# Moving two choosing matmuls of a sigmoid attention and mixture-of-depths kernel: the first sequence's to an earlier gap, the seventh's behind two products

## The chip, the cores and the metric

The kernel runs on one core of a Trainium2 chip. Its time is the device time of that core in microseconds. Three runs of the kernel before gave 466.89, 468.31 and 469.23 us; the median is 468.31 us. All arithmetic is in 32-bit floats.

The engines are named as in the profile: PE is TensorE (matmuls; PEld are its weight loads), DVE is VectorE, ACT is ScalarE, POOL is GpSimd, SP is SyncE, which only issues transfers. Each engine works through its own list of instructions in the order in which the program emits them, and waits where an operand or a buffer isn't ready.

## The reference

There are B=8 sequences of S=448 tokens, with 12 heads of 64. Attention with a sigmoid instead of a softmax gives x, one row of D=768 numbers for each token. Then a gate scores each token, the 128 tokens of each sequence with the highest scores go through a two-layer network, and the others are passed on as they are.

```python
scores = scale * np.matmul(q, k.transpose(0, 1, 3, 2)) - np.log(S)
attn = 1.0 / (1.0 + np.exp(-scores))
x = np.matmul(attn, v)            # then (B,H,S,D) -> (B, S, H*D)
...
scores = np.einsum('bsd,d->bs', x, w_gate)
out = x.copy()
for b in range(B):
    top_idx = np.argpartition(-scores[b], capacity)[:capacity]   # capacity 128
    xe = x[b, top_idx]
    h = np.maximum(xe @ w1, 0.0)  # w1: 768 x 1024
    ye = h @ w2                   # w2: 1024 x 768
    g = 1.0 / (1.0 + np.exp(-scores[b, top_idx]))
    out[b, top_idx] = x[b, top_idx] + g[:, None] * ye
```

## The kernel before

**Attention.** Four heads make a group, three groups a sequence, two groups a step: 12 steps `s`, so that sequence b ends in step (3b+2)//2. A step has seven units `n`. `unit(s, n)` (L287) computes a piece of the scores with 32 matmuls into two of PE's accumulation banks, and ACT takes them through the sigmoid. `values(s, n)` (L327) multiplies with v, in four parts: the first in unit 6 of the step itself, the others in the gaps after units 0, 1 and 2 of the next step. Its results stand in two banks `o0` and `o1`; after the last part `take` (L360) has DVE transpose them into `x_b`, four transposes for a step. In steps 1 to 3 unit 4 uses `o0` and `o1` for its scores too, between two steps' outputs. There are two further banks `psc`, which units use otherwise.

**Choosing the tokens.** `gate_part` (L370) multiplies x by the gate's weights and sums, four DVE operations for a group. When a sequence's three groups are done, `gate(b)` (L389) adds them up and POOL writes the 448 scores to memory (`scores`); `spread(b)` (L411) has POOL read them back to every partition (`rep`). `ranking(b)` (L667) compares every score with all others on DVE, ten operations in all, and `place` builds the matrix `hot` from the ranks. `choose(b)` (L438), the *choosing matmuls*, multiplies `hot` with the tokens' numbers and scores: four matmuls, eight PE instructions, into one bank. `fetch(b)` (L447) has DVE take the numbers (`idx`) and the scores (`got`) from that bank, and POOL gathers the chosen rows from `out` with an indirect transfer. The rows of the sequence were written to `out` before that by four stores on SP (`store`, L379), which `routed` (L649) places; those of sequence 0 are emitted at (2, 4), (2, 5.5), (2, 6) and (3, 0), step and unit.

**The network.** `turn_rows` (L468) turns the gathered rows round on PE. The two layers are computed for pairs of sequences in seven products each instead of eight (Strassen's scheme): `first` (L509) has 12 matmuls for a product, 24 PE instructions, and its sums (L532 and others) are DVE's.

**Order.** Nothing is planned by a scheduler: `stream` (L762) emits every instruction, so each engine's order is the program's. `gap(s, n)` (L684) holds what follows unit n: parts of `values`, then the network's work from the table `WORK`, then what `put` has left in `late`, then in gap 3 the second group's gate products and `gate`. For sequence 0 the scores are spread at (2, 4), the ranking is at (3, 1), and choice and fetch at (3, 5); for sequence 1 `gate` is in gap (3, 3), the spread at (3, 4) and the ranking at (4, 1), ahead of step 3's transposes in gap (4, 2). After unit 5 of steps 1 to 3 `keep_busy` (L319) has PE do some matmuls whose result nobody uses, into the bank that `open_outs` takes for the step's outputs.

**Banks.** `banks("o")` (L76) gives `o0` and `o1` in turn, `banks("any")` a `psc` bank and an `o` bank in turn, so that among four allocations each bank comes once. An allocation waits until the bank's last reader is done.

**The tail.** `rest` (L711) follows the last step. It emits the last parts of `values` with their transposes, the choice and fetch for sequence 6, products 6 and 7 of the third pair, the last group's gate products, `gate(7)`, the spread, the sums of products 6 and 7, then products 4, 5 and 3, second-layer products, `ranking(7)`, and so on to the end.

Of the kernel before, what the change touches and what calls it, by code (L numbers as in the profile page):

```python
# [17 lines left out]
def kernel(  # L18
# [22 lines left out]
    NG = H // 4  # L41
    NQ = B * NG
    NS = NQ // 2
# [32 lines left out]
    def banks(which):  # L76
        if which == "any":
            turns[1] ^= 1
            which = "psc" if turns[1] else "o"
        if which == "psc":  # L80
            return ps_sc.tile([P, 2, 512], F32, name="psc")
        if which == "o":
            turns[0] ^= 1
            which = turns[0]
        return ps_o[which].tile([P, 2, 512], F32, name=f"o{which}")
# [107 lines left out]
    def attn_tile(pr, slot):  # L193
        return attnp.tile([P, 2, S], F32, name=f"attn{pr}_{slot}")

    def lend(m, key, slot):


        halves = []
        for pr in range(2):  # L200
            if slot == "raw":
                t = raw.tile([P, TB * Dh], F32, name=f"raw_{'kq'[pr]}")[:, :QW // 2]
            elif slot == "turned":
                t = head.tile([P, 2, TB, TT], F32, name=f"{'kq'[pr]}T")
                t = t.rearrange("p e r t -> p (e r t)")[:, :QW // 2]
            else:
                t = attn_tile(pr, slot).rearrange("p a s -> p (a s)")[:, :QW // 2]
            nc.sync.dma_start(out=t, in_=sums[m, key][:, pr * QW // 2:(pr + 1) * QW // 2])
            halves.append(t)
        lent[m, key] = halves  # L210
# [104 lines left out]
    def open_outs(s):  # L315
        if s not in outs:
            outs[s] = [banks(0), banks(1)]

    def keep_busy(s):  # L319


        open_outs(s)
        for _ in range(3 if s == 3 else 4):
            nc.tensor.matmul(outs[s][0][:, 0, :HP * TT], iden,  # L324
                             wg_b.rearrange("p h t -> p (h t)"), start=True, stop=True)

# [43 lines left out]
    def gate_part(i):  # L370
        b, g = divmod(i, NG)
        for hp in range(2 * g, 2 * g + 2):
            tmp = moe.tile([P, TB, TT], F32, name="scr")
            nc.vector.tensor_tensor(  # L374
                out=tmp, in0=x_tiles[b][:, :, hp, :],
                in1=wg_b[:, hp:hp + 1, :].to_broadcast([P, TB, TT]), op=ALU.mult)
            nc.vector.tensor_reduce(out=gate_parts[b][:, :, hp], in_=tmp, axis=AX.X, op=ALU.add)  # L377

    def store(b, parts=range(4)):  # L379

        view = out[b].rearrange("(t r) (h a d) -> a t r h d", r=TB, a=4, d=TT)
        for a in parts:
            nc.sync.dma_start(out=view[a], in_=x_tiles[b][a * TT:(a + 1) * TT])

    def rows_to(b):

        return out[:b + 1].rearrange("b s d -> (b s) d")
# [50 lines left out]
    def choose(b, ps=None):  # L438

        if ps is None:  # L440
            ps = banks("o")[:, 0]
        for c in range(NC):
            nc.tensor.matmul(ps[:CAP, :2], st[b]["hot"][:, c, :CAP], who[b % 2][:, c, :],  # L443
                             start=(c == 0), stop=(c == NC - 1))
        return b, ps

    def fetch(b, ps):  # L447
        n = CAP
        idx = moe.tile([P, 1], I32, name="idx", bufs=5)
        nc.vector.tensor_scalar(out=idx[:n], in0=ps[:n, 0:1], scalar1=float(b * S),  # L450
                                scalar2=None, op0=ALU.add)
        got = moe.tile([P, 1], F32, name="got", bufs=4)
        nc.vector.tensor_copy(got[:n], ps[:n, 1:2])
        if b == B - 1:
            xe = attn_tile(0, f"u{NU - 1}").rearrange("p a s -> p (a s)")[:, :D]
        else:
            xe = moe.tile([P, D], F32, name="xe", bufs=3)
        nc.gpsimd.indirect_dma_start(
            out=xe[:n], out_offset=None, in_=rows_to(b),
            in_offset=bass.IndirectOffsetOnAxis(ap=idx[:n, 0:1], axis=0))  # L460
        st[b].update(idx=idx, xe=xe, picked=got)
# [3 lines left out]
    def bank(where):  # L465
        return banks(where)[:, 0]
# [163 lines left out]
    def begin(item, where="o"):  # L630

        m, p, key = item
        return (first if m == 1 else second)(p, key, where)

    def finish(item, args):
        (first_sums if item[0] == 1 else second_sums)(*args)

    def do(item, where="o"):
        if item[0] == "t":
            turn_rows(item[1], where)  # L640
        else:
            finish(item, begin(item, where))
# [3 lines left out]
    def put(s, n, fn, *args):  # L646
        late.setdefault((s, n), []).append((fn, args))

    def routed(b):  # L649

        s = (NG * b + NG - 1) // 2 + 1
        if s == NS:
            return
        put(s, 4, spread, b)
        if b < 2:

            parts = ((4, 0), (4, 1.5), (4, 3), (4, 4)) if b else (
                (2, 4), (2, 5.5), (2, 6), (3, 0))
            for a, at in enumerate(parts):
                put(*at, store, b, (a,))  # L660
        else:
            put(s, 4, store, b)
        put(s + 1, 1, ranking, b)
        if s + 1 < NS:
            put(s + 1, NU - 2, lambda b: fetch(*choose(b)), b)

    def ranking(b):  # L667
# [4 lines left out]
    def gates(i):  # L672
        gate_part(i)
        b, g = divmod(i, NG)
        if g == NG - 1:
            st[b] = {}
            waiting.append(b)

    def turned_next(s):

        m, x = WORK.get((s, 3), ((None, 0),))[0][:2]
        return m == "t" and x % 2 == 1

    def gap(s, n):  # L684
        if n < 3 and s > 0:
            values(s - 1, n + 1)
            if n == 2:
                turns[0] = 1
                for i, (m, key) in enumerate(LENT.get(s, ())):
                    lend(m, key, f"d{(s + 1) % 2}{i}")  # L690
                if not turned_next(s):
                    gates(2 * s - 2)
        for item in WORK.get((s, n), ()):
            do(item)
        if n == 3 and turned_next(s):
            gates(2 * s - 2)
        if n == 4 and turned_next(s):
            gate(waiting.pop())
            gates(2 * s - 1)
        if n == NU - 1 and s < NS:  # L700
            values(s, 0)
        for fn, args in late.pop((s, n), ()):
            fn(*args)
        if n == 3 and s > 0 and not turned_next(s):
            if waiting:
                gate(waiting.pop())
            gates(2 * s - 1)
            if waiting:
                gate(waiting.pop())

    def rest():  # L711


        for n in range(3):
            gap(NS, n)
        p, b = NP - 2, B - 1
        fetch(*choose(b - 1))
        for key, slot in (((2, 6), "d10"), ((2, 7), "d11")):
            lend(*key, slot)
        work = [(item, begin(item, "any")) for item in ((1, p, 6), (1, p, 7))]  # L720
        gates(2 * NS - 1)

        store(b, (0, 1))
        gate(waiting.pop())
        spread(b, nc.sync)
        store(b, (2, 3))
        for item, args in work:
            finish(item, args)
        for key in (4, 5):
            do((1, p, key), "any")  # L730
        first_sums(*begin((1, p, 3), "any"), sums_too=(5, 6))
        work = {key: begin((2, p, key), "any") for key in (2, 1, 4)}
        ranking(b)
        tile5 = banks("any")
        work[5] = second(p, 5, ps=tile5[:, 0])
        chosen = choose(b, tile5[:, 1])
        second_sums(*work[2])
        hidden_sum(p, 7)
        work[6] = begin((2, p, 6), "any")
        fetch(*chosen)  # L740
        second_sums(*work[1])
        hidden_sum(p, 3)
        work[7] = begin((2, p, 7), "any")
        for key in (4, 5, 6, 7):
            second_sums(*work[key])
        do(("t", b - 1), "any")
        do((2, p, 3), "any")
        p += 1
        for item in ((1, p, 1), ("t", b), (1, p, 2)):
            do(item, "any")  # L750
        work = [((1, p, key), begin((1, p, key), "any")) for key in (3, 6, 7)]
        for item, args in work[1:]:
            finish(item, args)
        first_sums(*work[0][1], sums_too=())
        for key in (4, 5):
            do((1, p, key), "any")
        for m in (5, 6, 7, 3):
            hidden_sum(p, m)
        for key in (1, 2, 6, 5, 3, 7, 4):
            do((2, p, key), "any")  # L760
# [76 lines left out]
```

## Time and profile before

One execution under the profiler spans 467.6 us.

| Engine | busy us | share of the span |
|---|---|---|
| PE, matmuls | 451.3 | 97% |
| PE, weight loads | 281.9 | 60% |
| DVE | 293.3 | 63% |
| ACT | 181.8 | 39% |
| POOL | 32.7 | 7% |

The transfers: 63.28 MB are read and 20.46 MB written, 179 GB/s over the span. On the chain of work that ended last PE has 85%, DVE 8% and transfers 3%.

How to read it: a row of the groups or the timeline gives the line of the kernel, the engine, the operation and the tiles as out<-in, then how often (x) and how long. "Idle before <-" says how long the engine had stood still and whose event ended that. Busy shares are means over stages of different kinds; what a change in one stage is worth is read from that stage. The windows view gives for a stretch of time the busy microseconds of each engine with the number of instructions, then the clock that was granted to PE (1.00 is full speed), the share of the transfer engines, and GB/s. Times in a view count from the start of the span.

### The profile page before, as it was taken

To read this page: it belongs to the slowest core of one execution; us is meant where nothing else is said; L and a number is where in the kernel's file an instruction comes from. 1 tells how busy PE (TensorE), PEld (TensorE's weight loads), DVE (VectorE), ACT (ScalarE), POOL (GpSimd) and SP (SyncE) were. 2 spreads that over 40 slices of the span, in tenths; PEclk is the share of its full clock that TensorE was granted. 3 is DMA by queue.
4 is the path that set the end of the run, shared out by engine and by line. 5 is a ranking of instruction groups with operands and counts; after the bars stand their busy time and mean duration, and the time that the engine had idled before them with its cause. 6 is when DMAs were issued, how large, how long until landed. Compare 5 with 4: busy or idle time off the path is not lost.

```text
span 467.6 us, 14444 instructions
## 1 busy us (share of the span) xinstructions
PE 451.3 (97%) x6412; PEld 281.9 (60%) x6412; DVE 293.3 (63%) x631; ACT 181.8 (39%) x237; POOL 32.7 (7%) x54
## 2 busy tenths in 40 slices
PE   8999999979999999999999999999999998999994
PEld 3464745434576755576456764676465738869952
DVE  4308769985642895984643795894742858685372
ACT  3846464624545345324445435324255520102000
POOL 6000000010000000010010000010010001001001
PEclk9999999979999999999999999999999998999998
DMA  8897997989753995994764973993823999611001
GB/s 269 220 313 185 342 347 149 264 197 302 165 193 116 207 192 185 204 215 153 173 227 148 153 202 118 228 213 132 220 102 98 222 181 328 106 34 69 2 0 67
DMA packets 128334, 84.67 MB, mean 181 GB/s; under 512 B 97600, under 2 KB 112064, under 8 KB 128272
## 3 DMA queue, kind: packets, MB, share of 16 engines
q1 hardware_dynamic: 126288, 75.84, 62.2%
q0 software_dynamic: 1984, 7.91, 5.7%
q8 instruction: 50, 0.82, 0.8%
q14 instruction: 12, 0.10, 0.1%
HBM read 63.28 MB, written 20.46 MB: 179 GB/s over the span
## 4 chain that ended last, share of the span: by engine, by line
PE 85%; DVE 8%; DMA 3%; issue 1%; ACT 1%; POOLq 0%; DVEq 0%; ACTq 0%
PE o L351 26%; PE psc L303 23%; PE o L519 13%; PE o L584 11%; PE psc L519 4%; PE psc L584 3%; DVE x_b L366 2%; PE o L303 2%; DMA scores<-total 1%; DVE gate_p L377 1%; DVE scr L374 1%; PE o L775 1%; PE o L443 1%; DMA rep<-scores 1%; PE o L324 1%
## 5 line engine op out<-in xcount | busy, mean ns | idle before, releaser
L303 PE MATMUL psc<-qT,kT 32*64 32x448 f32 x2496 | 155.1, 546 | 0.9 <-ACT attn_u L311 0.9
L311 ACT ACTIVATE attn_u<-psc,bias_s 128x896 f32<-128x896 f32 x86 | 81.9, 1004 | 94.6 <-PE psc L303 94.5
L351 PE MATMUL o<-attn_u,raw_v 32*64 32x448 f32 x960 | 107.8, 536 | 0.8 <-ACT o L354 0.8
L351 PE MATMUL o<-attn_d,raw_v 32*64 32x448 f32 x960 | 106.8, 536 | 0.4 <-ACT o L354 0.4
L303 PEld LDWEIGHTS psc<-qT,kT 32*64 32x64 f32 x2496 | 65.2, 133 | 56.4 <-issue 36.0
L311 ACT ACTIVATE attn_d<-psc,bias_s 128x896 f32<-128x896 f32 x70 | 66.7, 1003 | 47.9 <-PE psc L303 47.9
L366 DVE STREAM_TRANSPOSE x_b<-o 128x448 f32<-128x448 f32 x48 | 26.9, 618 | 81.5 <-PE o L351 77.3
L351 PEld LDWEIGHTS o<-attn_u,raw_v 32*64 32x64 f32 x960 | 45.6, 132 | 20.4 <-issue 12.5
L351 PEld LDWEIGHTS o<-attn_d,raw_v 32*64 32x64 f32 x960 | 43.9, 132 | 18.8 <-issue 14.8
L519 PEld LDWEIGHTS o<-rows_t,w_sb 128*128 128x128 f32 x264 | 30.4, 192 | 4.5 <-issue 1.4
L519 PEld LDWEIGHTS o<-rows_t,attn_d 128*128 128x128 f32 x264 | 30.3, 192 | 3.9 <-DVE scr L374 1.4
L519 PE MATMUL o<-rows_t,w_sb 128*128 128x128 f32 x264 | 31.9, 278 | 0.4 <-DVE rows_t L486 0.3
L519 PE MATMUL o<-rows_t,attn_d 128*128 128x128 f32 x264 | 31.6, 277 | 0.3 <-DVE rows_t L492 0.3
L377 DVE TENSOR_REDUCE gate_p<-scr 128x14 f32<-128x448 f32 x48 | 29.8, 621 | 1.7
L374 DVE TENSOR_TENSOR scr<-x_b,wg_b 128x448 f32<-128x448 f32 x48 | 29.5, 615 | 1.0
L595 DVE SCALAR_TENSOR_TENSOR xe<-o,gate,xe 128x384 f32<-128x384 f32 x37 | 21.1, 611 | 13.4 <-PE o L584 13.3
L278 DVE STREAM_TRANSPOSE kT<-raw_k 128x384 f32<-128x384 f32 x46 | 23.4, 548 | 7.5 <-PE psc L303 3.9
L584 PE MATMUL o<-attn_d,hidden 128*128 128x384 f32 x80 | 27.7, 494 | 0.0
L532 DVE TENSOR_TENSOR hidden<-o,hidden 128x512 f32<-128x512 f32 x24 | 16.0, 687 | 17.9 <-PE o L519 17.7
L535 ACT ACTIVATE hidden<-hidden 128x512 f32<-128x512 f32 x12 | 7.6, 630 | 49.9 <-DVE hidden L532 49.9
L422 DVE TENSOR_SCALAR_CACHE_REDUCE scr<-rep,who 128x448 f32<-128x448 f32 (+1 forms) x32 | 21.5, 671 | 8.6 <-DMA rep<-scores 7.6
L584 PE MATMUL o<-w_sb,hidden 128*128 128x384 f32 x72 | 24.7, 491 | 0.0
(112 smaller groups left out, 476.4 us busy)
## 6 DMA issues: line engine op xcount, KB each, us to landing
attn_d<-sum SPq DMA_DIRECT2D x42, 384.0 KB, 5.5
out_dram<-x_b SPq DMA_DIRECT2D x32, 336.0 KB, 7.7
raw_k<-in_k_dram SPq DMA_DIRECT2D x23, 448.0 KB, 5.3
raw_q<-in_q_dram SPq DMA_DIRECT2D x23, 448.0 KB, 5.9
raw_v<-in_v_dram SPq DMA_DIRECT2D x40, 192.0 KB, 8.1
w_sb<-in_moe_w_dram SPq DMA_DIRECT2D x6, 768.0 KB, 10.9
sum<-hidden SPq DMA_DIRECT2D x6, 768.0 KB, 6.3
rep<-scores POOLq DMA_DIRECT2D x7, 224.0 KB, 4.9
```

The source lines that it names most:

```text
L278: nc.vector.transpose(kT[i][:, e, :HK], sk[:, e, :HK].rearrange("p (m c) d -> p c m d", c=NF))
L303: nc.tensor.matmul(psc[h // 2][y * Dh:(y + 1) * Dh, h % 2, :S], kT[2 * s + x][d, e, r:r + 2, :].rearrange("d r t -> d (r t)"), qT[2 * s + ...
L311: nc.scalar.activation(a, psc[pr][:, :, :S], AF.Sigmoid, bias=bias_s, scale=QK_SCALE)
L351: nc.tensor.matmul(o[x][j * Dh:(j + 1) * Dh, pr, :S], w, a[rows, j, :], start=(n == 0 and c == 0), stop=(n == 3 and c == NF - 1))
L366: nc.vector.transpose(x_tiles[b][:, :, 2 * g + pr, :], outs[s][x][:, pr, :S].rearrange("p (r t) -> p r t", t=TT))
L374: nc.vector.tensor_tensor(out=tmp, in0=x_tiles[b][:, :, hp, :], in1=wg_b[:, hp:hp + 1, :].to_broadcast([P, TB, TT]), op=ALU.mult)
L377: nc.vector.tensor_reduce(out=gate_parts[b][:, :, hp], in_=tmp, axis=AX.X, op=ALU.add)
L422: nc.vector.tensor_scalar(out=junk[:n], in0=rep[:n], scalar1=own, scalar2=0.0, op0=ALU.is_gt, op1=ALU.add, accum_out=above[:n, c:c + 1])
L519: nc.tensor.matmul(ps[:, f, :n], w((t * FH + f) * P, P), x[:, t, :n], start=(t == 0), stop=(t == KH - 1))
L532: nc.vector.tensor_tensor(out=dst, in0=a, in1=b, op=ALU.add)
L584: nc.tensor.matmul(ps[:n, :DH], h[:, t, :n], w(t * DH, DH), start=(t == 0), stop=(t == FH - 1))
L595: nc.vector.scalar_tensor_tensor(out=xe[:n, cols], in0=ps[:n, :DH], scalar=st[b]["gate"][:n, 0:1], in1=xe[:n, cols], op0=ALU.mult, op1=ALU ...
```

## The change

Two choices move, and with them what belongs to them.

1. Sequence 0 (in step `FIRST`, which is 3): choice and fetch go from gap (3, 5) to gap (3, 3). Within that gap they come first; the first group's gate products `gates(4)`, which stood in gap (3, 2) after the transposes, now come after them, then the second group's and `gate(1)` as before. `keep_busy(3)` has four matmuls instead of three.
2. Sequence 6, in `rest`: the choice comes after products 6 and 7 have been begun instead of before them, and takes its bank from the common rotation ("any") instead of from the `o` pair. The fetch follows it.

```diff
-        for _ in range(3 if s == 3 else 4):
+        for _ in range(4):
             nc.tensor.matmul(outs[s][0][:, 0, :HP * TT], iden,
...
-        if s + 1 < NS:
+        if 0 < b and s + 1 < NS:
             put(s + 1, NU - 2, lambda b: fetch(*choose(b)), b)
...
+    FIRST = NG // 2 + 2
...
-                if not turned_next(s):
+                if not turned_next(s) and s != FIRST:
                     gates(2 * s - 2)
         for item in WORK.get((s, n), ()):
             do(item)
-        if n == 3 and turned_next(s):
+        if n == 3 and s == FIRST:
+            fetch(*choose(0))
+        if n == 3 and (turned_next(s) or s == FIRST):
             gates(2 * s - 2)
...
         p, b = NP - 2, B - 1
-        fetch(*choose(b - 1))
         for key, slot in (((2, 6), "d10"), ((2, 7), "d11")):
             lend(*key, slot)
         work = [(item, begin(item, "any")) for item in ((1, p, 6), (1, p, 7))]
+        fetch(*choose(b - 1, bank("any")))
         gates(2 * NS - 1)
```

## The prediction

> **What bounds the kernel now.** I read the page's first two parts, then the waits of the tensor engine, the windows around its longest wait, the timelines of GpSimd and VectorE there, and last the chain of the tail. On the page:
>
> ```profile
> PE 451.3 (97%) x6412; PEld 281.9 (60%) x6412; DVE 293.3 (63%) x631; ACT 181.8 (39%) x237; POOL 32.7 (7%) x54
> PEclk9999999979999999999999999999999998999998
> ```
>
> TensorE (PE) is busy for 97% of the span; a gain can come only from its few waits and from the slices whose clock digit is below 9. The waits of PE (total, times, longest) name two at the two places that the change touches:
>
> ```profile
> PE o L324 <- DVE got L453: 3.8, 1, 3.8
> ...
> PE o L443 <- DVE x_b L366: 1.5, 1, 1.5
> ```
>
> The first is sequence 0's choice in step 3: `keep_busy` reuses the bank that holds the result, and VectorE (DVE) takes the result late. The second is sequence 6's choice in the tail, waiting for the last step's transposes. Windows around the first, with the granted clock before the DMA share:
>
> ```profile
> 92.00:96.00 4.00, 0.83 (x8) 0.75 (x7) 3.66 (x14) 2.10 (x3) 0.40 (x1) 0.99 0.75 115
> 96.00:100.00 4.00, 3.32 (x22) 2.39 (x30) 3.96 (x9) 0.00 (x0) 0.69 (x2) 0.50 0.84 198
> 100.00:104.00 4.00, 4.00 (x64) 1.50 (x56) 3.68 (x6) 1.77 (x2) 1.10 (x1) 0.66 1.01 254
> ```
>
> PE stands still from 92.9 to 96.7 and then works at half clock until 102.8 (0.66 over the last window). DVE is full here: 3.66, 3.96 and 3.68 of 4. DVE's timeline shows where `idx` stands, and that DVE later waits, 2.32 us for `rep` of sequence 1 and 4.25 us before step 3's transposes:
>
> ```profile
> 96.31 0.16 DVE L450 TENSOR_SCALAR idx<-o 128x1 int32<-128x1 f32 x1
> ...
> 106.84 0.68 DVE L422 TENSOR_SCALAR_CACHE_REDUCE scr<-rep,who 128x448 f32<-128x448 f32 x1 [2.32 <-DMA rep<-scores]
> ...
> 117.76 2.24 DVE L366 STREAM_TRANSPOSE x_b<-o 128x448 f32<-128x448 f32 x4 [4.25 <-DMA out_dram<-x_b]
> ```
>
> GpSimd's timeline holds the row that decides my forecast: the order of its three transfers.
>
> ```profile
> 95.60 0.53 POOL L402 DMA_DIRECT2D scores<-total  x1 [19.84 <-DVE by_token L404]
> 99.07 0.56 POOL L414 DMA_DIRECT2D rep<-scores  x1 [2.94 <-DMA scores<-total]
> 100.12 1.10 POOL L458 DMA_INDIRECT xe<-out_dram,idx  x1 [0.50 <-DMA raw_k<-in_k_dram]
> ```
>
> The gather (L458) reads sequence 0's rows from `out`, so it needs all four of its stores. The DMA view of 94.9 to 97.9 shows when the fourth moves:
>
> ```profile
> DMA packets 2778, 0.35 MB, mean 117 GB/s; under 512 B 2778, under 2 KB 2778, under 8 KB 2778
> ```
>
> That is one store: 336 KB in runs of 128 bytes, 2688 packets. It has left the queue only by 97.9; with a few tenths for the landing I take 98.3. In the tail the chain reads:
>
> ```profile
> 388.32 1.02 PE o L443 x8
> 389.35 4.41 PE psc L519 x24
> 393.76 2.68 PE o L519 x24
> ```
>
> The first product after the wait takes 4.41 us, the next 2.68: half clock again, 1.7 us lost.
>
> **What the Trainium skill says.** "TensorE: Matmul & The Clock Gate", Part 1: a free-running window of about 3.4 us without work halves PE's clock, a busy one restores it. The trace agrees in kind (0.50 after a wait of 3.8 us), yet here 1.5 us with small gaps was enough in the tail. "DMA: Bandwidth & Descriptors", Anatomy of one DMA: a transfer's semaphore wait happens on the issuing sequencer, before dispatch. So a gather that waits for its stores holds every later GpSimd transfer; the 3.84 us that PE lost is DVE's version of the same. The same page, Queues, rings and completion order: each ring's descriptors are consumed in order, and a completion mark lands after the earlier writes of its engine. No view separates that, but the tail has a `scores` transfer issued at 396.3 with a gather of 392.06 in flight, and I use it below.
>
> **Step 3, part by part.** *Choosing matmuls to the third gap.* Eight PE instructions, 0.8 to 1.05 us, move from 91.8 to 87.6. Their input `hot` is ready (85.59+0.69), and their bank is free after two transposes (86.30+1.15=87.45). Unit (3,4) writes the same bank and must now wait until `idx` and `got` have read it. These follow the four transposes (end 88.5), so unit (3,4) starts near 88.9 instead of resuming at 88.59: +0.35 us.
>
> *Result ahead of the gate products.* `idx` and `got` (0.08 us each in the stream) go from 96.3 to 88.7. The four gate operations (2.5 us) stay behind them, so DVE's total is unchanged and `turn(8)` ends near 98.9 as before (98.6).
>
> *Fourth keep-warm matmul.* Two more PE instructions: eight took 1.50 us in step 1, so +0.4 us.
>
> *What PE gains.* The wait (3.84) and half of 6.1 us at half clock (3.05), less 0.35, 0.4 and some 0.1 of waiting for ScalarE before unit (3,6): 6.0 us. PE would reach `turn_rows(0)`, now at 119.05, at about 112.9. But that takes bank 0, which holds step 3's outputs. Their transposes stand on DVE behind ranking 1, and ranking 1 waits for `rep` of sequence 1.
>
> *What the moved fetch costs.* It issues a gather too, and that now stands first on GpSimd, ahead of `scores` and `rep` of sequence 1. It is ready at 88.9 except for the stores: start 98.4, 1.1 us long, so `scores` goes out at 99.9 instead of 95.6. The gather takes 3.8/5.5/9.4 us to land (min/median/max); the DMA engines are full, I take 6: 104.4. `scores` in the same queue lands at 105.3 (bounds 102.8, which is 99.9 plus the old 2.9, and 107; in the tail it took 4.4). `rep` is issued 0.5 later, 105.8, and takes 4.1 (sequence 0, chain) to 7.7 (this stage before); 5.5 taken, so 111.3 instead of 106.8. Ranking takes 6.7 (106.84 to 113.5): 118.0. Two transposes: 119.2. `turn_rows(0)` at 119.3: the six microseconds are used up, +0.25.
>
> *Clock.* PE then idles 112.9 to 119.3, longer than before, so it resumes at half clock. Of the 3.4 to 6.8 us at half clock, 3.4 to 6 fall on work; half of that, about 2.4 us, is lost again. Sum of step 3: +2.6 us. With the smallest bounds (`rep` at 107.5) it is -1.5, with the largest (116) about +8.
>
> **Tail, part by part.** Removed: PE's 1.5 us wait and the 1.7 us of half clock. Products 6 and 7 start at 386.9 and end at 392.3 (2.68 each), the choice at 393.1. Before, the choice and both products ended at 396.4: PE is 3.3 ahead.
>
> Added: two waits. `idx` on DVE now waits for the choice, 391.65 to 393.1, and the last step's gate products and gate 7 queue behind it. Those took 5.25 us, from 391.76 to the first of the following rows; now they run from 393.4 to 398.65:
>
> ```profile
> 397.04 0.69 DVE L532 TENSOR_TENSOR hidden<-psc,hidden 128x512 f32<-128x512 f32 x1
> 397.83 1.29 DVE L532 TENSOR_TENSOR hidden<-o,hidden 128x512 f32<-128x512 f32 x2
> ```
>
> So the sum of product 6 is finished at 399.4 instead of 397.7. And the banks rotate: the order was choice o0, 6 psc, 7 o1, 4 psc, 5 o0, 3 psc. It becomes 6 psc, 7 o0, choice psc, 4 o1, 5 psc, 3 o0. Product 5 now needs the bank of product 6, free at 399.4, while PE is there at 393.1+2.7=395.8. PE waits 3.6 us. Products 5 and 3 end at 404.8, where 404.35 stood before: +0.45, and DVE's ranking 7 starts at 407.0 for 406.65. An idle stretch of 3.6 us should halve the clock again: 0 to 1.7 us, 1.25 taken. Tail +1.7 (0.3 to 2.5). The delay of 1.6 us for gather 6, `scores` 7 and `rep` 7 is hidden: `rep` lands near 405.6, before ranking starts; the gather is used at 420. SP's own queue keeps its order.
>
> **Sum.** +2.6+1.7=+4.3 us against the span of 467.6. The profiled execution (469.52) is 1.2 above the median of the timed ones; I carry the difference over: 468.3+4.3, about 472.5.
>
> **Rivals.**
> 1. *Even.* The gather lands in 4 to 4.5 us and `rep` in 4: ranking 1 starts at about 108, step 3 gives -1.5, the tail +0.4 to +1.7: 467 to 469. For it: the quickest gather took 3.8 us, the median `rep` 4.9. Against: in 100 to 104 the DMA share is 1.01, and `rep` took 7.7 here.
> 2. *Faster (the other side).* `scores` 1 isn't held, because the gather needn't wait for the fourth store or the stores land earlier. Place: GpSimd's queue at 95.6. Ranking 1 then starts at 106.8, DVE frees bank 0 at 114.7, PE gains 4.3 less a little clock, and with an even tail: 464.5. It decides once ranking 1 starts before about 108. Against: the gather's rows are written by that store, and GpSimd's waits at L458 list a store (`DMA out_dram<-x_b`, 4.2 us, once).
> 3. *Bank wait absent.* If product 5 doesn't wait, the tail gives -3 and the sum is near even or, with rival 2, 461. Against: the rotation, counted above.
> 4. *Much slower.* Gather and `rep` both slow (8 and 7.7): 477.
>
> **Numbers.** Forecast 0.57; even 0.20; faster (2 and 3 together) 0.14; much slower 0.09. A measurement of this kernel tells about 0.5% (2.3 us) from no change. Faster 0.14, same 0.20, slower 0.66. The range 465.5 to 476.5 leaves out about 0.10 below and 0.07 above.
>
> **What would show it.** Right: no 3.8 us wait at L324; on GpSimd the gather near 98.4 and `scores` near 99.9, `rep` after 105; ranking 1 on DVE starting near 111; PE idle before `turn_rows(0)` (L480) for some 6 us, waiting for x_b; in the tail the first product 2.7 us long, and PE waiting some 3.6 us for a `hidden` sum of L532. Wrong: ranking 1 at 108 or earlier, a short PE wait at L480, no wait within the five products, or the clock staying full through both gaps.

## The result

The changed kernel is slower: 474.2 us (median of four runs, 472.99 to 475.09) against 467.6 us for the kernel before (four runs), a ratio of 1.0139 with a 95% interval of 1.0094 to 1.0184; of 467.6 us that is 4.4 to 8.6 us. The profiled execution spans 472.69 us, 5.07 more than that of before, which at 469.52 us of device time was a little slower than each of the four runs. The page of the changed kernel:

```profile
PE 449.6 (95%) x6414; PEld 284.6 (60%) x6414; DVE 293.0 (62%) x631; ACT 182.0 (38%) x237; POOL 32.8 (7%) x54
```

The work is the same but for the fourth `keep_busy` matmul (two PE instructions); PE has two points less of the span. Its waits (total, times, longest) say where:

```profile
PE o L480 <- issue: 10.0, 1, 10.0
PE o L519 <- DVE hidden L532: 2.0, 1, 2.0
...
PE o L303 <- DVE got L453: 0.4, 1, 0.4
```

The two waits that the change aimed at, 3.8 us at L324 and 1.5 us for the last step's transposes at L443, are gone, at the price of 0.4 us before unit (3, 4). In their place stand 10.0 us before `turn_rows(0)` and 2.0 us in the tail. "issue" means that the view found no releaser for the first; the timelines of GpSimd and DVE supply it. GpSimd's, with the transfers in their new order:

```profile
98.70 1.05 POOL L458 DMA_INDIRECT xe<-out_dram,idx  x1 [22.74 <-DMA raw_k<-in_k_dram]
99.74 0.58 POOL L402 DMA_DIRECT2D scores<-total  x1
108.14 0.56 POOL L414 DMA_DIRECT2D rep<-scores  x1 [7.82 <-DMA scores<-total]
```

GpSimd stood still for 22.74 us in front of the gather, while `idx` had been ready for the last ten of them; `scores` left 4.1 us later than before (95.60) and `rep` 9.1 later (99.07). The other 5.0 us of `rep`'s delay are the transfer of `scores`, which took 7.9 us to land instead of 2.9 and landed 0.3 us after the gather. DVE's timeline:

```profile
88.64 0.16 DVE L450 TENSOR_SCALAR idx<-o 128x1 int32<-128x1 f32 x1
...
115.19 0.68 DVE L422 TENSOR_SCALAR_CACHE_REDUCE scr<-rep,who 128x448 f32<-128x448 f32 x1 [10.87 <-DMA rep<-scores]
...
121.79 2.23 DVE L366 STREAM_TRANSPOSE x_b<-o 128x448 f32<-128x448 f32 x4
```

`idx` comes 7.7 us earlier, as meant. But ranking 1 waits 10.87 us for `rep` (2.32 before), and the transposes follow directly after it, without the slack of 4.25 us that stood there. PE, done with unit (4, 3) at 113.1, gets its bank at 123.1. Windows over that stretch, the granted clock ahead of the DMA share:

```profile
116.00:120.00 4.00, 0.00 (x0) 0.00 (x0) 3.82 (x11) 0.00 (x0) 0.00 (x0) 0.50 1.08 280
120.00:124.00 4.00, 0.94 (x5) 0.97 (x6) 3.90 (x11) 0.00 (x0) 0.00 (x0) 0.50 0.92 139
```

The choice of sequence 1, at 130.29 in the chain of before, stands at 134.53: step 3 has cost 4.24 us. In the tail the chain reads:

```profile
391.12 2.88 PE psc L519 x24
393.99 2.68 PE o L519 x24
396.67 0.80 PE psc L443 x8
...
404.96 4.42 PE o L519 x24
```

Products 6 and 7 run at once and at full clock (2.88 and 2.68 us), then the choice. The long row, 4.42 us, is now product 3, after a wait of 2.0 us; that wait ends with the sum of product 7 on DVE, and DVE had waited 1.49 us for the choice:

```profile
397.50 0.16 DVE L450 TENSOR_SCALAR idx<-psc 128x1 int32<-128x1 f32 x1 [1.49 <-PE psc L443]
...
403.62 2.08 DVE L532 TENSOR_TENSOR hidden<-o,hidden 128x512 f32<-128x512 f32 x3
```

From the last `values` matmul to the end of choice 7 PE needs 29.53 us, 28.76 before: the tail has cost 0.77. With 4.24 that is 5.0 of the 5.07 us between the spans; it is 1.1%, within the interval of the timed ratio.

### The profile page after: what moved, and what is told of

It reads as the page before. It is cut to its first block, busy times and chain, and to the rows that moved or that the text cites. A ratio compares the mean times of both kernels' runs of the same rounds, so it can differ in the third digit from the quotient of the medians.

```text
span 472.7 us, 14446 instructions
## 1 busy us (share of the span) xinstructions
PE 449.6 (95%) x6414; PEld 284.6 (60%) x6414; DVE 293.0 (62%) x631; ACT 182.0 (38%) x237; POOL 32.8 (7%) x54
## 4 chain that ended last, share of the span: by engine, by line
PE 89%; DVE 5%; issue 3%; DMA 1%; ACT 1%; POOLq 0%; DVEq 0%; ACTq 0%
PE o L351 27%; PE psc L303 26%; PE o L519 12%; PE o L584 11%; PE psc L584 3%; PE psc L519 3%; PE o L303 3%; PE o L443 1%; PE o L779 1%; PE o L324 1%; DVE gate_p L377 1%; DVE scr L374 1%; DVE x_b L366 1%; DMA out_dram<-xe,idx 1%; PE o L480 0%
## 5 line engine op out<-in xcount | busy, mean ns | idle before, releaser
L303 PE MATMUL psc<-qT,kT 32*64 32x448 f32 x2496 | 154.8, 543 | 0.6 <-ACT attn_u L311 0.6
L351 PE MATMUL o<-attn_u,raw_v 32*64 32x448 f32 x960 | 107.6, 536 | 0.8 <-ACT o L354 0.8
L303 PEld LDWEIGHTS psc<-qT,kT 32*64 32x64 f32 x2496 | 65.9, 132 | 55.7 <-issue 35.1
L519 PEld LDWEIGHTS o<-rows_t,attn_d 128*128 128x128 f32 x264 | 30.3, 192 | 3.9 <-DVE scr L374 1.4
L519 PE MATMUL o<-rows_t,attn_d 128*128 128x128 f32 x264 | 31.6, 277 | 0.3 <-DVE rows_t L492 0.3
L595 DVE SCALAR_TENSOR_TENSOR xe<-o,gate,xe 128x384 f32<-128x384 f32 x39 | 22.1, 610 | 11.9 <-PE o L584 11.8
L278 DVE STREAM_TRANSPOSE kT<-raw_k 128x384 f32<-128x384 f32 x46 | 23.4, 547 | 8.2 <-DMA raw_k<-in_k_dram 4.5
L532 DVE TENSOR_TENSOR hidden<-o,hidden 128x512 f32<-128x512 f32 x26 | 17.3, 687 | 17.9 <-PE o L519 17.6
L519 PEld LDWEIGHTS o<-rows_t,w_sb 128*128 128x128 f32 x216 | 24.8, 192 | 4.2 <-issue 1.4
L519 PE MATMUL o<-rows_t,w_sb 128*128 128x128 f32 x216 | 26.3, 278 | 0.4 <-DVE rows_t L486 0.2
```

The costliest lines, as they stand in the source:

```text
L278: nc.vector.transpose(kT[i][:, e, :HK], sk[:, e, :HK].rearrange("p (m c) d -> p c m d", c=NF))
L303: nc.tensor.matmul(psc[h // 2][y * Dh:(y + 1) * Dh, h % 2, :S], kT[2 * s + x][d, e, r:r + 2, :].rearrange("d r t -> d (r t)"), qT[2 * s + ...
L351: nc.tensor.matmul(o[x][j * Dh:(j + 1) * Dh, pr, :S], w, a[rows, j, :], start=(n == 0 and c == 0), stop=(n == 3 and c == NF - 1))
L519: nc.tensor.matmul(ps[:, f, :n], w((t * FH + f) * P, P), x[:, t, :n], start=(t == 0), stop=(t == KH - 1))
L532: nc.vector.tensor_tensor(out=dst, in0=a, in1=b, op=ALU.add)
L595: nc.vector.scalar_tensor_tensor(out=xe[:n, cols], in0=ps[:n, :DH], scalar=st[b]["gate"][:n, 0:1], in1=xe[:n, cols], op0=ALU.mult, op1=ALU ...
```

## The experiments

In each a ratio is to the kernel before on the same chip, with its 95% interval in brackets. The median of that kernel was 467.9 us for `e1` to `e4`, 466.4 for `e5` to `e8` and 468.5 for `e9` and `e10`, so an expectation in microseconds, made from the first chip, lies some 1.5 us too high for the second group. A ratio is not the quotient of the two medians; the two differ most for `e3_gather_late` (0.9933 and 0.9958).

**Each part alone.** `e1_step3_only` takes the tail's edit back, `e2_tail_only` the edit of step 3:

```diff
 # e1_step3_only, against the changed kernel
+        fetch(*choose(b - 1))
         for key, slot in (((2, 6), "d10"), ((2, 7), "d11")):
...
-        fetch(*choose(b - 1, bank("any")))
```

> Theory: the change's loss arises in step 3, because the moved gather holds scores and rep of sequence 1 on GpSimd. Then this part alone costs +4.2 us of the +5.05 between the two spans: about 471.8 us, rep of sequence 1 landing near 115, PE idle for some 10 us before turn_rows(0). Rival: step 3 comes out even and the tail carries the loss: 467 to 468.5.

Measured: 472.23 us, ratio 1.0103 (1.0072 to 1.0134). `rep` is read at 112.93 and PE idles 7.7 us before `turn_rows(0)`; choice 1 starts 2.6 us later than before in this execution, in which `rep` landed 2.3 us earlier than in the changed kernel's. The times differ by more than the profiles, because the profiled execution of before was 1.7 us slower than this group's median.

> Theory: in the tail the removed wait and half clock (3.1 us) are given back by a wait of about 2 us for the sum of product 7 ahead of product 3, with half clock after it: +0.8 us, 468.4, not to be told from no change by the times, but PE waiting 2 us at L519 in the profile. Rival 1: the tail alone gains its 3 us (464.5), and what was lost came from step 3. Rival 2: it carries the loss, +4 us.

Measured: 468.4 us, ratio 1.0015 (1.0001 to 1.0029), and PE waits 2.0 us at L519 for `hidden`. So the loss is step 3's, and the tail gives back what it gains, or 0.1% more.

**The gather alone moved back.** `e3_gather_late` keeps choice, `idx` and `got` in gap (3, 3) and issues the gather after `rep` of sequence 1 (tail as before). The lines not shown make a function `gather_rows` of the gather:

```diff
...
+        if b == 0:
+            put(s + 1, NU - 2, gather_rows, b)
...
-            fetch(*choose(0))
+            fetch(*choose(0), gather=False)
```

> Choice, idx and got of sequence 0 stay in gap (3, 3), the gather alone is issued after rep of sequence 1, at (3, 5); tail as before the change. Theory (order on GpSimd): scores goes out at about 95.8 again, ranking 1 starts near 107 and ends at 113.7, turn_rows(0) at about 115 after 2 us of idle PE; 4 us gained less up to 1.7 for the clock: 463.5 to 465. Rival (full transfer engines or DVE's new order delay rep, whatever GpSimd's order): ranking 1 at 112 or later, 469 or more.

Measured: 465.88 us, ratio 0.9933 (0.9902 to 0.9963): slower has become faster. GpSimd's timeline of this kernel, and the row of DVE's with ranking 1:

```profile
95.32 0.53 POOL L402 DMA_DIRECT2D scores<-total  x1 [19.73 <-DVE by_token L404]
101.46 0.56 POOL L414 DMA_DIRECT2D rep<-scores  x1 [5.62 <-DMA raw_v<-in_v_dram]
102.52 1.05 POOL L465 DMA_INDIRECT xe<-out_dram,idx  x1 [0.50 <-DMA raw_h<-in_v_dram]
```

```profile
107.58 0.68 DVE L422 TENSOR_SCALAR_CACHE_REDUCE scr<-rep,who 128x448 f32<-128x448 f32 x1 [3.89 <-DMA rep<-scores]
```

`scores` leaves at 95.3 again and ranking 1 starts at 107.6; PE idles 3.0 us before `turn_rows(0)` instead of 10.0. GpSimd's order is the cause of the delay. The median is 1 to 2 us above what I expected. The clock goes with that: the two fastest runs, at 460.86 and 462.94 us, had a mean granted clock of 0.997 and 0.998, the run at 465.91 had 0.989. The profile is that of the run at 462.94, so it shows a better case than the median.

**Was it the stores?** `e5_stores_early` leaves the gather in front, but emits the four stores of sequence 0 together:

```diff
-                (2, 4), (2, 5.5), (2, 6), (3, 0))
+                (2, 4), (2, 4), (2, 4), (2, 4))
```

> The changed step 3 with the tail of before; all four stores of sequence 0 are emitted at (2, 4) instead of between (2, 4) and (3, 0), so they land near 90. Theory (the gather in front of scores does harm because it stands waiting for the stores): the gather goes out before 92, scores at about 95.8, ranking 1 starts at 106 to 108, turn_rows(0) at about 115 after some 2 us of idle PE: 463 to 466. Rival 1 (a gather ahead in the queue delays scores by itself, stores or not): scores lands after 103 and ranking 1 starts after 110, 468 or more. Rival 2 (the stores now delay the loads for turn(8)): DVE waits at L278 near 96 and PE with it.

Measured: 464.96 us, ratio 0.9968 (0.995 to 0.9986). The gather leaves at 89.0, `scores` at 95.2, and ranking 1 starts at 107.5; PE idles 3.2 us. So a gather in front of `scores` did harm by standing there until 98.7, and its wait was for the stores. Rival 1 falls for this order: `scores` landed at 101.5 and ranking 1 was on time; its 6.3 us of transfer are a little above the 5.6 of `e3_gather_late`, where no gather is ahead. Rival 2 falls too: DVE does not wait at L278 near 96.

The gather of this run landed at 97.8, well before `scores`. Where the gather is issued directly in front of `scores`, it may hold it in flight as well. In all five such traces (the changed kernel, `e1`, `e4`, `e7`, `e9`) `scores` landed 0.2 to 0.3 us after the gather and 6.5 to 7.9 us after it left; in the six where the gather follows, it took 2.9 to 5.6 us. But the `scores` of sequence 0, with no gather ahead, took 6.0 to 7.8 us in all twelve traces, so something other than a gather, such as full transfer engines, can do the same. No run here tells the two apart.

**Who held PE?** `e4_ranking_after` leaves GpSimd's bad order as it is and puts ranking 1 behind step 3's transposes on DVE (tail as before):

```diff
-        put(s + 1, 1, ranking, b)
+        put(s + 1, 2 if b == 1 else 1, ranking, b)
```

> GpSimd's order as in the changed kernel, but ranking 1 stands on DVE behind step 3's transposes and first gate products; tail as before the change. Theory (PE waits only because the transposes queue behind ranking 1 on DVE): rep still lands near 115, but turn_rows(0) runs at about 113 and the full 6 us are gained: about 461.6. Rival (PE would meet the late rep elsewhere, at the choice of sequence 1 in gap (4, 5)): the idle time moves there and the time is 466 or more.

Measured: 461.87 us, ratio 0.9888 (0.9859 to 0.9916). DVE's timeline:

```profile
111.54 2.24 DVE L366 STREAM_TRANSPOSE x_b<-o 128x448 f32<-128x448 f32 x4 [7.63 <-PE o L351]
...
116.29 0.68 DVE L422 TENSOR_SCALAR_CACHE_REDUCE scr<-rep,who 128x448 f32<-128x448 f32 x1
```

`rep` lands at 115.5, as late as in the changed kernel (115.1), and nobody waits for it: the transposes and gate products fill the time. Choice 1 starts at 124.1, 6.2 us earlier than before. The full gain of step 3 was there; it was lost in DVE's queue, behind a ranking that waited.

**Result ahead of the gate products.** `e9_gates_first` is `e4_ranking_after` with `gates(4)` back in gap (3, 2), before `idx` and `got`:

```diff
-                if not turned_next(s) and s != FIRST:
+                if not turned_next(s):
                     gates(2 * s - 2)
...
-        if n == 3 and (turned_next(s) or s == FIRST):
+        if n == 3 and turned_next(s):
             gates(2 * s - 2)
```

> As e4_ranking_after, but the first group's gate products of step 3 go back ahead of idx and got, into gap (3, 2). Theory (unit (3, 4) writes the bank of the choice and waits for got): idx runs 2.5 us later, at about 91.2, PE waits some 2.5 to 3 us at L303 before unit (3, 4), and the time is 2.5 us above e4_ranking_after (its ratio 0.9888 becomes about 0.994), more if the wait halves the clock. Rival: ScalarE is still emptying unit (3, 3) and hides it, and nothing changes.

Measured: 467.06 us, ratio 0.9956 (0.9932 to 0.998), 0.0068 (3.2 us) above `e4_ranking_after`, which ran on another chip; the intervals do not touch. PE's timeline:

```profile
88.88 1.84 PE L443 MATMUL o<-who,hot 128*128 128x2 f32 x8 [2.38 <-DVE x_b L366]
92.55 3.21 PE L303 MATMUL o<-qT,kT 32*64 32x448 f32 x32 [1.83 <-DVE got L453]
```

PE waits 1.8 us for `got` at L303 instead of 0.4. The clock is at half there, but it is so from 88.7 on, before that wait: the choice already takes 1.84 us, for 1.02 in the changed kernel. In front of it stands a wait of 2.4 us for the transposes, which stood behind a ranking 0 that ended later, ahead of the edit. So the profile shows 1.4 us of the edit's cost, and does not show that the half clock is the edit's. By the times this part of the change earns its place.

**The tail.** `e6_tail_one` puts product 6 alone ahead of the choice, `e8_tail_sums_first` keeps the changed order on PE and puts the sums of products 6 and 7 ahead of `idx` on DVE (both with step 3 as before the change):

```diff
 # e6_tail_one, against the kernel before
-        fetch(*choose(b - 1))
         for key, slot in (((2, 6), "d10"), ((2, 7), "d11")):
             lend(*key, slot)
-        work = [(item, begin(item, "any")) for item in ((1, p, 6), (1, p, 7))]
+        work = [((1, p, 6), begin((1, p, 6), "any"))]
+        fetch(*choose(b - 1))
+        work.append(((1, p, 7), begin((1, p, 7), "any")))
```

> Step 3 as before the change; in the tail product 6 alone goes ahead of the choice, which keeps its bank of the o pair, and product 7 follows. Theory (the changed tail lost because idx and with it all of DVE's work waited 1.5 us for two products): idx runs at once after the first gate products, no wait for a sum at L519, and PE keeps 1.4 us, with the half clock 3 us: 465 to 466.5. Rival (any product ahead of the choice pushes the ranking of sequence 7 back): no gain, 467.5 to 469.

Measured: 464.16 us, ratio 0.9954 (0.9932 to 0.9977). The chain of its tail:

```profile
383.64 2.88 PE psc L519 x24
386.52 0.79 PE o L443 x8
387.31 2.79 PE o L519 x24
```

`idx` runs right after the first gate products and no product waits.

```diff
 # e8_tail_sums_first, against e2_tail_only
-        fetch(*choose(b - 1, bank("any")))
+        chosen = choose(b - 1, bank("any"))
+        for item, args in work:
+            finish(item, args)
+        fetch(*chosen)
         gates(2 * NS - 1)
...
-        for item, args in work:
-            finish(item, args)
```

> Step 3 as before the change; tail as changed, but the sums of products 6 and 7 stand on DVE ahead of idx, the gate products and gate 7. Theory (in the changed tail PE waits 2 us at product 3 because the bank of product 7 is read only after gate 7): that wait is gone, and instead scores and rep of sequence 7 come 1 to 2 us later, so the gain or loss is within 1.5 us of 468.4, and where PE waits later it is at the choice of sequence 7. Rival (the wait at product 3 has another cause, such as the weights from memory): PE still waits 2 us at L519.

Measured: 464.36 us, ratio 0.9947 (0.9929 to 0.9965), better than I expected: the wait at L519 is gone, so it was for the sum's place in DVE's queue and not for weights, and the later `scores` cost nothing. In `e6_tail_one` and here PE needs 25.59 us from the last `values` matmul to the end of choice 7, for 28.76 before.

**Both together.** `e7_both` is `e4_ranking_after` with the tail of `e6_tail_one`.

> The changed step 3 with ranking 1 behind the transposes (as in e4_ranking_after), together with product 6 ahead of the choice in the tail (as in e6_tail_one). Theory: the gains add, 461.9 less 1.4 (the tail's clock was already full there), about 460.5. Rival: the tail's gain is that of the clock alone, and nothing is added to 461.9.

Measured: 457.51 us, ratio 0.9807 (0.9772 to 0.9841), the fastest here, faster than both kernels. The gain is at least the sum of the two (0.9888 and 0.9954 make 0.9842 together). Its page:

```profile
PE 444.2 (97%) x6414; PEld 267.6 (59%) x6414; DVE 292.9 (64%) x631; ACT 181.6 (40%) x237; POOL 32.7 (7%) x54
PEclk9999999999999999999999999999999999999998
```

The clock is full until the last slice. `e10_both_gather_late` adds the late gather of `e3_gather_late` to it.

> As e7_both, with the gather of sequence 0 issued after rep of sequence 1. Theory (once the transposes no longer queue behind ranking 1, the late rep is hidden): rep lands 3 to 7 us earlier and the time stays that of e7_both, ratio 0.981 within 0.002. Rival (the late rep still costs at the choice of sequence 1): faster than e7_both by 0.5% or more.

Measured: 460.1 us, ratio 0.9819 (0.9796 to 0.9843), no difference from `e7_both` that the intervals tell. `rep` landed at 107.5 instead of 112.5. Once the transposes stand ahead, GpSimd's order costs less than these intervals can tell (some 0.3%).

What the fourth `keep_busy` matmul costs or gains by itself was not tested; every kernel with the changed step 3 has it.

## Why the prediction was right

The direction, the held queue in step 3 and a second wait in the tail were as forecast, and 474.2 us lies in the range. The forecast for the spans was +4.3 us, and they differ by 5.07; by the timed runs the loss is 4.4 to 8.6 us. That the sum came so near is in part luck: step 3 cost 4.24 us where 2.6 were forecast, the tail 0.77 where 1.7 were.

*Step 3, the gain.* PE reached the end of unit (4, 3) at 113.1 (112.9 forecast), and the wait before unit (3, 4) was 0.41 us (0.35).

*Step 3, the queue.* The gather started at 98.7 and `scores` at 99.7 (98.4 and 99.9). What was too small is the transfers' time: the gather took 8.6 us to land, 6 taken; `rep` left at 108.1, not 105.8, and was read 7.1 us after it left, 5.5 taken. So ranking 1 started 3.9 us later than forecast, and `turn_rows(0)` 3.8 later; PE idled for 10.0 us, not 6. That `scores` would land behind the gather was assumed, and it did, by 0.3 us, though the cause stays open (above). `e3_gather_late` and `e5_stores_early` confirm from two sides that the held queue is the cause of the loss, and `e4_ranking_after` that it reached PE through ranking 1.

*Step 3, the clock.* I charged 2.4 us for half clock and the stretch grew by 0.2: from `turn_rows(0)` to choice 1 PE needs 11.24 us before and 11.47 after, though 3.2 us of it ran at half clock. The missing term is the stop itself. In the kernel before PE is held up by ScalarE in that stretch, and after a stop ScalarE has caught up. `e3_gather_late`, which stopped for 3.0 us and kept its full clock, needs 9.98 us. So the half clock cost 1.5 us and the stop had saved 1.3. The two errors of step 3 cancel in part: 3.8 us too little for the queue, 2.2 too much for the clock.

*The tail.* The failed step is "Product 5 now needs the bank of product 6". PE's timeline has product 5, DVE's the first read of product 6:

```profile
400.08 2.84 PE L519 MATMUL psc<-rows_t,attn_d 128*128 128x128 f32 x24
```

```profile
402.90 0.69 DVE L532 TENSOR_TENSOR hidden<-psc,hidden 128x512 f32<-128x512 f32 x1
```

Product 5 ran from 400.1 to 402.9 without a wait, while the bank of product 6 wasn't read before 402.90; so it used the other `psc` bank, that of the choice, whose reader comes first in the program. The rule that among four allocations each bank comes once does not hold here. It looks as if the pool of two gives out first what is released first in the program, not what was allocated first; only this one case shows it. The wait came one product later, for the bank of product 7, and was 2.0 us instead of 3.6. `e8_tail_sums_first` shows the reason that was given, the sums behind gate 7 on DVE. At full clock the changed tail takes 27.91 us (`e2_tail_only`), the old one 27.14 (`e4_ranking_after`): 0.77 more, the same as between the two kernels with the clock at half in both. Forecast was +1.7. (Of that, 0.1 is a slip: in the chain of before product 3 ends at 404.48, not 404.35.)

*The rivals.* Rival 1 needed a gather of 4 to 4.5 us; it took 8.6. Rival 2 gave the decision point, ranking 1 starting before 108: `e3_gather_late` and `e5_stores_early` have it there and are faster by 0.7 and 0.3%. Rival 3 had no wait in the tail; there was one, a product later. Rival 4 asked for a gather of 8 us and a `rep` of 7.7 and put the time at 477. The gather was that slow, and `rep` took 6.9 to land; the relief from ScalarE and the shorter wait in the tail kept the loss smaller.

## What to carry to other kernels

When an operation moves forward, move in thought everything that it issues: here four matmuls moved well, and the gather that followed them stopped a queue in which two other transfers had to pass. Ask of each engine's queue what stands behind the newcomer and who waits for that; here the cure was to let work that was ready pass in front of work that waited, the transposes ahead of the ranking. A matmul hoisted ahead of a result pays only until the engine that reads the result runs dry: one product ahead of the choice gained 0.5%; two gained nothing, until their sums were put ahead of `idx` on DVE too, and then 0.5% as well.

## What the runs showed of the hardware

The traces record a granted clock of 1.0 or 0.5 and nothing between, and its changes within a run lie on a grid of 3.41 us: in the kernel before the clock was full for 26 such cells (88.75 us), half for 2, full for 84, half for 1 and full for 21. The grid has another phase in each run. That agrees with the free-running window of the Trainium skill ("TensorE: Matmul & The Clock Gate", Part 1). Its limit, a whole idle window, doesn't fit, as 1.50 us of 3.41 was enough in four runs.

How much of a cell PE stood idle can be counted from its matmuls. In the twelve traces, up to the end of PE's work, every cell at full clock that was idle for 60% or more was followed by half clock (15 cells), none idle for 40% or less was, and of ten between 44 and 56% five were. So the place of a wait on the grid counts as well as its length. The wait of 1.50 us before the choice of sequence 6 filled 44% of a cell each time; the clock fell to half for 3.41 us in the kernel before, in `e1_step3_only`, in `e5_stores_early` and in `e9_gates_first`, and didn't in `e3_gather_late` and `e4_ranking_after`. At this length it is a matter of chance. The wait of 2.04 us halved the clock in the changed kernel (60% of a cell) and didn't in `e2_tail_only` (55%). The wait of 2.97 us in `e3_gather_late` fell into two cells, 47 and 40%, and didn't; 3.22 us in `e5_stores_early` left one cell 84% idle and did.

The price of a half-clock cell in the tail is 28.76-27.14=1.6 us in the kernel before and 29.53-27.91=1.6 in the changed one. That is half of the 3.2 us that `e6_tail_one` takes off the tail; the other half is the wait.
